# A Fourier-and-mixer kernel: fold pieces in two quarters only, a new setup order, and finer last stores

## The chip, the cores and the metric

The kernel runs on 1 core of one Trainium2 chip. The metric is the device time of one launch in microseconds (us), smaller is better; it is the median of repeated runs. A profile is of one execution and has a span (first to last recorded event) that is a little shorter than the time of that execution.

## The reference

The input x is 8 batches of 3008 rows (tokens) by 256 features, in fp32. Its two-dimensional Fourier transform over rows and features is taken and its real part goes through one mixer block with weights over tokens and over channels:

```python
x = np.fft.fft(np.fft.fft(x, axis=1), axis=2).real
xt = x.transpose(0, 2, 1)
h = np.maximum(xt @ w_tok1, 0.0) @ w_tok2     # 3008 -> 256 -> 3008
u = x + h.transpose(0, 2, 1)
h2 = np.maximum(u @ w_ch1, 0.0) @ w_ch2       # 256 -> 1536 -> 256
return u + h2                                  # fp32
```

## The kernel before

**The work per batch.** The transform over 3008 rows is split into 64 times 47. `load_x` (L155) brings a batch in as `xp` and, gathered by an indirect DMA, as the mirrored rows `xm`. `fold` (L445) adds each row's mirror to it (`xp` add, L457) and makes even and odd halves over the features (`eo` add L461, `eo` subtract L463), in four parts of three pieces: 12 pieces a batch, all on VectorE; the first piece has two small ones beside it (L455, L456). `front` (L561) is a generator of the transform and the token mixing: `inner` and `outer` products into `z`, twelve `pw` products into `w` (L587, L588, combined on VectorE at L590), then in `rest` (L596) the products with the token weights `tok1` (L601, part 0 from `hp`, part 1 from `hq`), the sums of the two parts (`part_q` on ScalarE, `units` on VectorE), the relu into `uu`, and `third` (L631), which finishes the transform in `yt`. The chunk loop (L680) then makes, for each of six chunks of 512 tokens and two halves of 128 features, `pu` = token weights times `uu` in two products, and `ut` = `pu` + `yt` in one VectorE add (L704); the view `"p (b a) -> p a b"` turns the order of the tokens on the way.

**The channel part.** `mm1` (L728) multiplies a chunk of `ut` with the first channel weights (`wc1p` or its mirror `wc1m`) into twelve `pc` banks, and ScalarE writes the relu to `c1` (L739). The second channel product is done by `mm2_sums` (L764) in seven products of quarter size for eight; it needs block sums of `c1` (`block_sums`, L743, four adds for each half of the blocks) and of the weights (`wst`). It runs in four quarters s = 0 to 3, and its residuals (L762) are added to the output tile `osb` by VectorE, and by POOL at the end of quarters 0 and 3. Chunk 0 of batch 0 and the last chunk of an even batch and of the last batch take the plain path (`mm2`, L817: twelve products into `po` per 128 tokens).

**The order.** The schedule is written out by hand: each engine runs its instructions in the order of the program. Banks of PSUM come from three pools, `f` with three, `mm` with three and `o2` with two; setup code takes them in turn from a ring over all (`ps_any`, L79). The main loop (L930) goes over batches b, chunks c and quarters s; sub = 4c + s is the sub-step. In each it issues three `mm1` blocks of this chunk, some pieces of this batch's front (`own_plan`), some of the next one's (`nxt`, by `plan`), one quarter of `mm2` of the previous chunk, and by `fold_plan` a piece of the fold of batch b + 2 (for b = 1, of batch 2 and then 3). The inner function `now()` (L945) issues block sums: those of the previous chunk's second half at s = 0 and 1, of this chunk's first half at s = 2 and 3. In batch 0 `align_w2` copies the token weights into the aligned `w2p` on ScalarE, piece by piece; `early` is the fold of batch 1.

**The setup** (L874 to 914) makes the sine tables `tp` and `tq` (ScalarE), transposes them (`turn_in`, `turned_out`), reverses their rows (`turn_rows`), multiplies them with the token weights (`carried`, six groups for `hp`, six for `hq`), and meanwhile does batch 0's fold (`fold0`) and front (`zw0`, `mirrored` for the mirror column of `w`, then `rest(0)`). `filler(n)` issues n products of 128 columns whose result isn't used; `warm(24)` is the like, of 256 columns, at the start. DMAs for weights go out on POOL's queue (`gdma`, `gather`); outputs and the transposes of `ut` (`turn_u`) on SP's.

Of the kernel before, what the change touches and what calls it, by code (L numbers as in the profile page):

```python
# [41 lines left out]
def kernel(  # L42
# [24 lines left out]
    def ps_mm(name):  # L67
        return psum.tile([P, 512], FP32, tag="mm", name=name, bufs=3)

    def ps_out(name):  # L70
        return psum.tile([P, 512], FP32, tag="o2", name=name, bufs=2)
# [6 lines left out]

    def ps_any(name, dt=FP32, n=512):  # L79
        tag, bufs = next(ring)  # L80
        return psum.tile([P, n], dt, tag=tag, name=name, bufs=bufs)
# [176 lines left out]
    def turn_in(tab):  # L258
        pts = []
        for h in range(2):  # L260
            pt = ps_any("pt", FP16, 1024)
            for g in range(6):
                nc.tensor.transpose(out=pt[:, g * P:(g + 1) * P],
                                    in_=tab[:, 6 * h + g, :], identity=ident[:])
            pts.append(pt)
        return pts
# [5 lines left out]
    def turn(tab, tts, warm):  # L272
        turned_out(tts, turn_in(tab))
        filler(warm)
# [321 lines left out]
    def rest(b):  # L596
# [63 lines left out]
        else:  # L660
            third(0)
            yield
            pts = [ps_out("pt1") for _ in range(2)]
            for th in range(2):
                tok1(pts[th], th, 0)
            yield
            sqs = []
            for th in range(2):
                tok1(pts[th], th, 1)
                sqs.append(part_q(pts[th]))  # L670
            uvs = [units(pts[th], sqs[th]) for th in range(2)]
            relu(0, uvs[0], (0,))
            for h in range(2):
                nc.scalar.activation(out=uu[:, 1, 0, h, :], in_=uvs[1][:, h, :],
                                     func=AFT.Relu)
            for th in range(2):
                relu(th, uvs[th], (1, 2))
            yield
        uts = st["ut"] = []
        for c in range(NCH):  # L680
# [10 lines left out]
            uts.append(ut)  # L691
            for h in range(2):
# [124 lines left out]
    def mm2(b, c, c1, ks, box):  # L817
# [15 lines left out]
        for ct in range(NCT if n else 0):  # L833
            nc.tensor.matmul(po[0:n, o:o + D], lhsT=c1[:, ct, ks * P:ks * P + n],  # L834
                             rhs=wc2[:, ct, :],
                             start=(ct == 0), stop=(ct == NCT - 1))
        if ks % 2 == 1 or final:
# [9 lines left out]
        first = 2 if final and ks == 3 else 0  # L847
        if ks == 3 or (final and ks == 1):
            for i in range(2):
                nk = min(ks + 1, 3 if last and (i or n == 0) else 4)  # L850
                eng = nc.scalar if i and final else nc.sync
# [4 lines left out]
            if ks == 3 and last and b % 2:  # L856
                nc.sync.dma_start(
# [18 lines left out]
    turn(tp, tts_p, 16)  # L876
# [9 lines left out]
    turned_out(tts_q, turn_in(tq))  # L886
    for g2, e in enumerate((1, 1)):
        carried(tts_p, hp, g2, e)
    table_perm()
    take(own, 4)  # L890
    carried(tts_p, hp, 2, 0)
# [7 lines left out]
    carried(tts_q, hq, 0, 0)  # L899
    mirrored(state[0]["w"], ps_any("pt1"))  # L900
    own = front(0)
    carried(tts_q, hq, 1, 1)
    take(own, 1)
    carried(tts_q, hq, 2, 0)
    take(own, 1)
    carried(tts_q, hq, 3, 1, ps_mm)
    carried(tts_q, hq, 4, 0, ps_mm)
    carried(tts_q, hq, 5, 0, ps_mm)
    take(own, 3)
    tables_folded()  # L910
    filler(12)
# [14 lines left out]
    fold_plan = [[0] * 15 + [1] * 9] + [[0] * 10 + [1] * 12 + [0, 0]] * (BB - 1)  # L926
    fold_plan[1] = [1, 1, 1] + fold_plan[1][3:]
    prev = None
    turned_u = {(0, 0): turn_u(0, 0)}
    for b in range(BB):  # L930
# [3 lines left out]
        for c in range(NCH):  # L934
# [6 lines left out]
            for s in range(4):  # L941
# [13 lines left out]
                take(nxt, n // 2)  # L955
# [4 lines left out]
                if s == 2:  # L960
                    now()
                if b == 0 and sub < 16 and sub % 2:
                    align_w2(sub // 2)
                take(nxt, n - n // 2)
                if s == 1:
                    now()
# [55 lines left out]
```

## Time and profile before

| what | value |
|---|---|
| three runs, us | 606.51, 605.36, 606.27 (median 606.27) |
| profiled execution, us | 605.55 |
| its span, us | 603.8 |
| granted TensorE clock, mean | 1.00 |
| DMA moved, MB (mean GB/s) | 56.53 (94) |
| fold pieces: `xp` add L457, `eo` add L461, `eo` subtract L463, mean ns | 768, 695, 618 (28 each) |
| block sum L753, mean ns of its four forms | 598, 564, 567, 554 (84 each) |
| TensorE busy in 0 to 33, 33 to 100, 100 to 530, 530 to 604 us | 23.98, 65.78, 430.00, 69.21 |
| VectorE busy in the same | 26.50, 53.52, 330.13, 43.67 |

PE is TensorE's matmul, PEld its weight load, DVE VectorE, ACT ScalarE, POOL GpSimd, SP SyncE; a q behind a name is the engine's queue of DMA issues and semaphore waits. A line of the page's group list has the source line, the engine, the operation, output<-input by the program's names, the shape and the count, then the busy time and the mean ns of one. A line of the timeline has the start in us, the duration in us of the whole group of like instructions, engine, line, operation, output<-input, shape, count, and in brackets how long the engine stood idle before it and which instruction's end released it. Matmuls are pipelined: the duration of one (219 ns for 128 columns) is longer than the time from its start to the next one's. Row names leave numbers out, so that `c` is `c1`, `pt` is `pt1` and `wc` is `wc2`.

### The profile page before, as it was taken

Reading aid. Unit: us, or ns where it says so; the run is one execution under the profiler, and the core shown is the slowest. Engines: PE = TensorE matmul, PEld = TensorE weight load, DVE = VectorE, ACT = ScalarE, POOL = GpSimd, SP = SyncE. Lnnn points to the kernel's source line nnn. Section 1 sums busy time; section 2 is a strip of 40 time slices with the busy share of each in tenths; the row PEclk is TensorE's granted clock in tenths of the full one; section 3 lists DMA queues with packets and bytes.
Section 4 is the critical chain, followed back from the end, with each engine's and each line's share of the span. In section 5 each row is a group of like instructions: output and inputs, shape, how many; then the busy total and the mean of one; then the engine's idle time right before and its main releaser. Section 6 shows DMA issues by size and latency. Waiting matters only on the chain.

```text
span 603.8 us, 15712 instructions
## 1 busy us (share of the span) xinstructions
PE 589.0 (98%) x6323; PEld 421.3 (70%) x6323; DVE 453.8 (75%) x1022; ACT 436.7 (72%) x983; POOL 146.0 (24%) x234
## 2 busy tenths in 40 slices
PE   4999999999999999999999999999999999999996
PEld 3846677666877677767777667766777677766675
DVE  8788697669796798657988589756989666766572
ACT  8776985777777776687777777777776877767772
POOL 7500412311341121311223212401221121111131
PEclk9999999999999999999999999999999999999999
DMA  9994761693467223952429332482232424232423
GB/s 153 210 202 117 111 104 37 113 157 57 66 113 143 53 63 80 150 72 65 96 46 169 87 71 55 94 163 53 55 88 44 82 53 93 51 71 65 85 60 99
DMA packets 86665, 56.53 MB, mean 94 GB/s; under 512 B 54928, under 2 KB 83536, under 8 KB 85840
## 3 DMA queue, kind: packets, MB, share of 16 engines
q1 hardware_dynamic: 78048, 37.84, 32.9%
q0 software_dynamic: 8320, 17.49, 16.9%
q8 instruction: 49, 0.80, 0.5%
q14 instruction: 24, 0.20, 0.1%
q10 hardware_dynamic: 224, 0.20, 0.1%
HBM read 34.98 MB, written 24.64 MB: 99 GB/s over the span
## 4 chain that ended last, share of the span: by engine, by line
PE 93%; DVE 3%; ACT 3%; issue 0%; DVEq 0%; POOL 0%; POOLq 0%
PE pc L736 39%; PE px L777 23%; PE py L777 9%; PE pu L696 7%; PE po L834 4%; PE pt L604 4%; PE pz L509 1%; PE pq L636 1%; PE py L636 1%; PE pw L588 1%; PE pw L587 1%; DVE sb L753 1%; ACT c L739 0%; PE pw L551 0%; DVE osb L762 0%
## 5 line engine op out<-in xcount | busy, mean ns | idle before, releaser
L739 ACT ACTIVATE c<-pc 128x512 f16<-128x512 f32 (+1 forms) x572 | 295.8, 594 | 38.1 <-PE pc L736 20.1
L762 POOL TENSOR_TENSOR osb<-osb,rt 128x256 f32<-128x256 f32 x84 | 79.5, 946 | 367.7 <-DVE osb L762 360.6
L736 PE MATMUL pc<-ut,wc1p 128*128 128x512 f16 x576 | 140.5, 379 | 0.0
L777 PEld LDWEIGHTS <-c 128*128 128x128 f16 x2016 | 121.4, 98 | 21.6 <-issue 1.8
L736 PE MATMUL pc<-ut,wc1m 128*128 128x512 f16 (+1 forms) x576 | 134.9, 370 | 0.0
L704 DVE TENSOR_TENSOR ut<-pu,yt 128x512 f16<-128x512 f32 (+1 forms) x96 | 64.6, 675 | 51.9 <-PE pu L696 51.7
L782 ACT ACTIVATE m<-px 128x256 f32<-128x256 f32 x126 | 48.5, 385 | 68.2 <-PE px L777 44.2
L777 PEld LDWEIGHTS <-sb 128*128 128x128 f16 x1512 | 90.0, 98 | 10.4 <-issue 0.7
L736 PEld LDWEIGHTS <-wc1p 128*128 128x128 f16 x576 | 52.2, 98 | 49.2 <-issue 2.6
L736 PEld LDWEIGHTS <-wc1m 128*128 128x128 f16 x576 | 52.9, 98 | 46.5
L777 PE MATMUL px<-wst,c 128*128 128x128 f16 x1008 | 70.9, 219 | 0.6 <-DVE c L753 0.6
L777 PE MATMUL px<-wc,c 128*128 128x128 f16 x1008 | 63.1, 219 | 0.3 <-DVE osb L762 0.3
L753 DVE TENSOR_TENSOR sb<-sb,c 128x768 f16<-128x768 f16 x84 | 50.3, 598 | 2.9
L305 ACT ACTIVATE z<-pz 128x480 f16<-128x480 f32 (+1 forms) x60 | 40.0, 672 | 16.9 <-PE pz L509 11.1
L762 DVE TENSOR_TENSOR osb<-py,m 128x256 f32<-128x256 f32 x84 | 35.2, 419 | 21.0 <-ACT m L782 19.5
L696 PE MATMUL pu<-w2p,uu 128*128 128x512 f16 (+1 forms) x168 | 49.8, 379 | 0.0
L753 DVE TENSOR_TENSOR sb<-c 128x768 f16<-128x768 f16 x84 | 47.4, 564 | 2.0 <-ACT c L739 2.0
L753 DVE TENSOR_TENSOR sb<-c,sb 128x768 f16<-128x768 f16 x84 | 47.6, 567 | 0.0
L753 DVE TENSOR_TENSOR c<-c 128x768 f16<-128x768 f16 x84 | 46.5, 554 | 0.0
L590 DVE SCALAR_TENSOR_TENSOR w<-alt,pw 128x131 f16<-128x131 f16 x84 | 29.4, 351 | 18.1 <-ACT w L305 17.4
L643 DVE TENSOR_TENSOR yt<-py,qs 128x512 f16<-128x512 f32 x48 | 30.9, 686 | 15.7 <-ACT qs L639 14.9
L777 PE MATMUL py<-wst,sb 128*128 128x128 f16 x504 | 35.2, 219 | 0.1
(184 smaller groups left out, 681.0 us busy)
## 6 DMA issues: line engine op xcount, KB each, us to landing
out_dram<-osb SPq DMA_DIRECT2D x83, 256.0 KB, 3.6
xp<-in_x_dram POOLq DMA_DIRECT2D x16, 272.0 KB, 5.5
out_dram<-osb SPq DMA_DIRECT2D x11, 192.0 KB, 3.2
xp<-in_x_dram POOLq DMA_DIRECT2D x16, 127.5 KB, 6.3
rt<-ut SPq DMA_TRANSPOSE x96, 3.9
w2s<-in_moe_w_tok_dram POOLq DMA_DIRECT2D x1, 1504.0 KB, 14.5
w1p<-in_moe_w_tok_dram POOLq DMA_DIRECT2D x4, 192.0 KB, 7.8
wc<-in_moe_w_ch_dram POOLq DMA_DIRECT2D x1, 768.0 KB
```

What stands on the lines that cost most here:

```text
L305: nc.scalar.activation(out=out_, in_=in_, func=AFT.Copy)
L590: nc.vector.scalar_tensor_tensor(out=w[:, g, 0:131], in0=alt[:], scalar=pw[:, 131:132], in1=pw[:, 0:131], op0=AT.mult, op1=AT.add)
L604: nc.tensor.matmul(pt[:, o:o + n], lhsT=hw[:, g, th * P:th * P + P], rhs=w[:, g, f:f + n], start=(g == 0), stop=(g == NG - 1))
L643: nc.vector.tensor_tensor(out=yt[:, h, CW * c:CW * c + CW], in0=py[:], in1=qs[:], op=op)
L696: nc.tensor.matmul(pu[:, 0:n], lhsT=uu[:, th, int(minus), h, :], rhs=w2_cols(b, c)[:, th], start=(th == 0), stop=(th == 1))
L704: nc.vector.tensor_tensor(out=ut[:, h, 0:n].rearrange("p (a b) -> p a b", b=64), in0=pu[:, 0:n].rearrange("p (b a) -> p a b", b=64), in1=y ...
L736: nc.tensor.matmul(pc[:, 0:n], lhsT=wc[:, h, ct * P:(ct + 1) * P], rhs=ut[:, h, 0:n], start=(h == 0), stop=(h == 1))
L739: nc.scalar.activation(out=c1[:, ct, 0:n], in_=pc[:, 0:n], func=AFT.Relu)
L753: nc.vector.tensor_tensor(out=o, in0=x, in1=y, op=op)
L762: eng.tensor_tensor(out=o, in0=x, in1=y, op=AT.add)
L777: nc.tensor.matmul(o[:, t], lhsT=a(k)[:, f:f + P], rhs=w(k), start=(first and t == 0 and k == 0), stop=(k == HC - 1), skip_group_check=True)
L782: nc.scalar.activation(out=m[:, i], in_=pa[:, 0], func=AFT.Copy)
```

## The change

1. **Setup order.** `tq` is transposed right after `tp`, into the two `o2` banks, which the ring then leaves out (`held`) until ScalarE has copied them; the 16 fillers there become 12 and 4, and the 12 before the main loop go. The first `hp` groups are evicted in a slightly different order. Groups 1 to 3 of `hq` now stand between `mirrored` and `third(0)`, groups 4 and 5 between `third(0)` and the first `tok1` products; some evictions change engine.
2. **Batch 0's token mixing and chunk 0.** ScalarE copies part 0 of `tok1` to `sp`, and VectorE subtracts and adds part 1 from PSUM. The four relus come in the order th 0, th 1. In chunk 0 `yt` is added in PSUM, by a product with the identity matrix whose output is written in the order `(b a)`, strided; VectorE and ScalarE then copy one half each to `ut`.
3. **Fold pieces.** `fold_plan` puts one piece at s = 0 and two at s = 1, none at s = 2 and 3; in batch 0 the pieces (2, 2, 1, 0, 2, 2) come at sub-steps 16 to 21. `load_x(b + 3)` comes at sub-step 22, `load_x(3)` at 1 of batch 1.
4. **Block sums.** At s = 1 `now()` comes right after `mm2`, ahead of the next front's pieces, and both of these come after `mm2`.
5. **Last stores.** In the last chunk the last 128 tokens are computed in two halves of 128 features, each with its residual at once; tokens of ks = 2 are stored by themselves, and the last store goes on ScalarE's queue.

```diff
@@ -76,8 +76,10 @@
     ring = cycle((("f", 3), ("mm", 3), ("o2", 2), ("f", 3), ("mm", 3), ("f", 3), ("mm", 3),
                   ("o2", 2)))
 
+    held = set()
+
     def ps_any(name, dt=FP32, n=512):
-        tag, bufs = next(ring)
+        tag, bufs = next(r for r in ring if r[0] not in held)
         return psum.tile([P, n], dt, tag=tag, name=name, bufs=bufs)
 
     def dram(t, offset, ap):
@@ -255,10 +257,10 @@
         return [stage.tile([P, NG * P], FP16, tag="tt", bufs=4, name="tt")
                 for _ in range(2)]
 
-    def turn_in(tab):
+    def turn_in(tab, pool=ps_any):
         pts = []
         for h in range(2):
-            pt = ps_any("pt", FP16, 1024)
+            pt = pool("pt", FP16, 1024)
             for g in range(6):
                 nc.tensor.transpose(out=pt[:, g * P:(g + 1) * P],
                                     in_=tab[:, 6 * h + g, :], identity=ident[:])
@@ -660,21 +662,27 @@
         else:
             third(0)
             yield
-            pts = [ps_out("pt1") for _ in range(2)]
+            uvs, sps = [], []
             for th in range(2):
-                tok1(pts[th], th, 0)
+                pt = ps_mm("pt1")
+                tok1(pt, th, 0)
+                sp = perb.tile([P, 130], FP32, tag="sp", name="sp", bufs=2)
+                nc.scalar.activation(out=sp[:], in_=pt[:, 0:130], func=AFT.Copy)
+                uv = perb.tile([P, 2, P], FP32, tag="uv", name="uv", bufs=2)
+                nc.vector.tensor_copy(out=uv[:, :, 0], in_=sp[:, 0:130:129])
+                sps.append(sp)
+                uvs.append(uv)
             yield
-            sqs = []
             for th in range(2):
-                tok1(pts[th], th, 1)
-                sqs.append(part_q(pts[th]))
-            uvs = [units(pts[th], sqs[th]) for th in range(2)]
-            relu(0, uvs[0], (0,))
-            for h in range(2):
-                nc.scalar.activation(out=uu[:, 1, 0, h, :], in_=uvs[1][:, h, :],
-                                     func=AFT.Relu)
+                pt = ps_out("pt1")
+                tok1(pt, th, 1)
+                for h, op in ((0, AT.subtract), (1, AT.add)):
+                    nc.vector.tensor_tensor(out=uvs[th][:, h, 1:P], in0=sps[th][:, 2:129],
+                                            in1=pt[:, 130:257], op=op)
             for th in range(2):
-                relu(th, uvs[th], (1, 2))
+                for h in range(2):
+                    nc.scalar.activation(out=uu[:, th, 0, h, :], in_=uvs[th][:, h, :],
+                                         func=AFT.Relu)
             yield
         uts = st["ut"] = []
         for c in range(NCH):
@@ -689,6 +697,25 @@
             elif n < CW:
                 nc.vector.memset(ut[:, :, n:CW], 0.0)
             uts.append(ut)
+            if (b, c) == (0, 0):
+                pus = [ps_f("pu") for _ in range(2)]
+                for h in range(2):
+                    nc.tensor.matmul(pus[h][:].rearrange("p (b a) -> p a b", b=64),
+                                     lhsT=ident[:],
+                                     rhs=yt[:, h, 0:CW].rearrange("p (a b) -> p a b", b=64),
+                                     start=True, stop=False)
+                for th in range(2):
+                    for h in range(2):
+                        nc.tensor.matmul(pus[h][:], lhsT=uu[:, th, 0, h, :],
+                                         rhs=w2_cols(b, c)[:, th],
+                                         start=False, stop=(th == 1))
+                for h in range(2):
+                    copy(1 - h, ut[:, h, :].rearrange("p (a b) -> p a b", b=64),
+                         pus[h][:].rearrange("p (b a) -> p a b", b=64))
+                for th in range(2):
+                    relu(th, uvs[th], (1, 2))
+                yield
+                continue
             for h in range(2):
                 minus = c >= 3
                 pu = ps_f("pu")
@@ -830,11 +857,17 @@
             box["po"] = ps_out("po")
         po = box["po"]
         o = D * (ks % 2)
-        for ct in range(NCT if n else 0):
-            nc.tensor.matmul(po[0:n, o:o + D], lhsT=c1[:, ct, ks * P:ks * P + n],
-                             rhs=wc2[:, ct, :],
-                             start=(ct == 0), stop=(ct == NCT - 1))
-        if ks % 2 == 1 or final:
+        w = P if final and ks == 3 else D
+        for d in range(0, D if n else 0, w):
+            for ct in range(NCT):
+                nc.tensor.matmul(po[0:n, o + d:o + d + w],
+                                 lhsT=c1[:, ct, ks * P:ks * P + n],
+                                 rhs=wc2[:, ct, d:d + w],
+                                 start=(ct == 0), stop=(ct == NCT - 1))
+            if final and ks == 3:
+                j, p = ((lower, lower), (upper, turned_))[d // w]
+                residual(nc.vector, osb[:, 3, j], po[:, o + d:o + d + w], rt[:, 3, p])
+        if ks % 2 == 1 and not final or final and ks < 3:
             src = po[:].rearrange("p (k d) -> p k d", k=2)
             parts = [(slice(0, P), 0, 2)] if n == P else [(slice(0, P), 0, 1),
                                                           (slice(0, n), 1, 2)]
@@ -844,17 +877,19 @@
                 ks_ = slice(ks - ks % 2 + k0, ks - ks % 2 + k1)
                 for j, p in ((lower, lower), (upper, turned_)):
                     residual(nc.vector, osb[r, ks_, j], src[r, k0:k1, j], rt[r, ks_, p])
-        first = 2 if final and ks == 3 else 0
-        if ks == 3 or (final and ks == 1):
+        first = ks if final and ks > 1 else 0
+        if ks == 3 or (final and ks):
             for i in range(2):
                 nk = min(ks + 1, 3 if last and (i or n == 0) else 4)
+                if nk == first:
+                    continue
                 eng = nc.scalar if i and final else nc.sync
                 eng.dma_start(
                     out=dram(out_t, (b * S + 8 * c + i + 2 * first) * D,
                              [[NQ * D, 64], [2 * D, nk - first], [1, D]]),
                     in_=osb[64 * i:64 * i + 64, first:nk, :])
             if ks == 3 and last and b % 2:
-                nc.sync.dma_start(
+                (nc.scalar if final else nc.sync).dma_start(
                     out=dram(out_t, ((b - 1) * S + NQ - 1) * D, [[NQ * D, 64], [1, D]]),
                     in_=osb[64:P, 3, :])
 
@@ -873,7 +908,11 @@
 
     warm(24)
     table3(tq, vq, (shift0[:], shift1[:]))
-    turn(tp, tts_p, 16)
+    held.add("o2")
+    turned_out(tts_p, turn_in(tp, ps_mm))
+    filler(12)
+    pts_q = turn_in(tq, ps_out)
+    filler(4)
     table_d()
     pieces = fold0()
     take(pieces, 5)
@@ -883,12 +922,12 @@
     take(own, 3)
     table_b()
     take(own, 3)
-    turned_out(tts_q, turn_in(tq))
-    for g2, e in enumerate((1, 1)):
+    turned_out(tts_q, pts_q)
+    held.clear()
+    for g2, e in enumerate((1, 1, 0)):
         carried(tts_p, hp, g2, e)
     table_perm()
     take(own, 4)
-    carried(tts_p, hp, 2, 0)
     turn_rows(tts_q, -1.0, 0)
     take(own, 3)
     carried(tts_p, hp, 3, 1)
@@ -896,19 +935,16 @@
     carried(tts_p, hp, 4, 0)
     take(own, 2)
     carried(tts_p, hp, 5, 1)
-    carried(tts_q, hq, 0, 0)
+    carried(tts_q, hq, 0, 1)
     mirrored(state[0]["w"], ps_any("pt1"))
     own = front(0)
-    carried(tts_q, hq, 1, 1)
+    for g2, e in ((1, 0), (2, 1), (3, 0)):
+        carried(tts_q, hq, g2, e)
     take(own, 1)
-    carried(tts_q, hq, 2, 0)
-    take(own, 1)
-    carried(tts_q, hq, 3, 1, ps_mm)
-    carried(tts_q, hq, 4, 0, ps_mm)
-    carried(tts_q, hq, 5, 0, ps_mm)
+    for g2, e in ((4, 1), (5, 0)):
+        carried(tts_q, hq, g2, e)
     take(own, 3)
     tables_folded()
-    filler(12)
     load_wc2()
     if BB > 1:
         x_tiles[1] = load_x(1)
@@ -923,8 +959,9 @@
                 [1, 1, 1, 0, 0, 1, 1, 0, 1, 1, 0, 0, 1, 1] + [0] * 10]
     own_plan += [[1, 1, 1, 0, 0, 1, 1, 0, 1, 1, 0, 0, 1, 1] + [0] * 10] * (BB - 2)
     early_plan = [0] * 4 + [2, 2, 1, 2, 1, 2, 2] + [0] * 13
-    fold_plan = [[0] * 15 + [1] * 9] + [[0] * 10 + [1] * 12 + [0, 0]] * (BB - 1)
-    fold_plan[1] = [1, 1, 1] + fold_plan[1][3:]
+    fold_plan = [[0] * 8 + [1, 2, 0, 0] * 4 for _ in range(BB)]
+    fold_plan[0] = [0] * 16 + [2, 2, 1, 0, 2, 2, 0, 0]
+    fold_plan[1] = [1, 2, 0, 0] + [0] * 4 + [0, 2, 0, 0] + [1, 2, 0, 0] * 2 + [1, 2, 1, 0]
     prev = None
     turned_u = {(0, 0): turn_u(0, 0)}
     for b in range(BB):
@@ -952,18 +989,17 @@
                 if s == 3:
                     now()
                 take(own, own_plan[b][sub])
-                take(nxt, n // 2)
+                first = 0 if s == 1 else n // 2
+                take(nxt, first)
                 if s == 0:
                     now()
                 if prev is not None:
                     mm2(*prev, s, pbox)
-                if s == 2:
+                if s in (1, 2):
                     now()
                 if b == 0 and sub < 16 and sub % 2:
                     align_w2(sub // 2)
-                take(nxt, n - n // 2)
-                if s == 1:
-                    now()
+                take(nxt, n - first)
                 if s == 2 and c + 1 < NCH:
                     turned_u[b, c + 1] = turn_u(b, c + 1)
                 if s == 3 and c + 1 == NCH and b + 1 < BB:
@@ -977,12 +1013,12 @@
                     if sub == 10:
                         x_tiles[2] = load_x(2)
                 if folds is not None and fold_plan[b][sub]:
-                    take(folds, 1)
-                    if b == 1 and sub == 2:
+                    take(folds, fold_plan[b][sub])
+                    if b == 1 and sub == 1:
                         x_tiles[3] = load_x(3)
                         folds = fold(3, [nc.vector] * 4)
-                    elif sub == 21 and b and b + 3 < BB:
-                        x_tiles[b + 3] = load_x(b + 3)
+                if sub == 22 and b and b + 3 < BB:
+                    x_tiles[b + 3] = load_x(b + 3)
             if c + 1 == NCH and b % 2 == 0:
                 pair(b, c1)
             prev, pbox = (b, c, c1), box
```

More of the change, by code (lines that the diff above doesn't have):

```diff
@@ L65, with ps_mm, ps_out @@
         tc.tile_pool(name="psump", bufs=1, space=bass.MemoryType.PSUM))
[L67 to L71, printed above, removed]
+    def ps_mm(name, dt=FP32, n=512):
+        return psum.tile([P, n], dt, tag="mm", name=name, bufs=3)
+    def ps_out(name, dt=FP32, n=512):
+        return psum.tile([P, n], dt, tag="o2", name=name, bufs=2)
     def ps_f(name, dt=FP32, n=512):
```

## The prediction

> **What bounds the kernel now.** I read the page first, its shares of busy time and then the chain that ended last:
>
> ```profile
> PE 589.0 (98%) x6323; PEld 421.3 (70%) x6323; DVE 453.8 (75%) x1022; ACT 436.7 (72%) x983; POOL 146.0 (24%) x234
> ...
> PEclk9999999999999999999999999999999999999999
> ...
> PE 93%; DVE 3%; ACT 3%; issue 0%; DVEq 0%; POOL 0%; POOLq 0%
> ```
>
> TensorE is busy 98% of the span and is 93% of the chain. By starts of neighbouring matmuls, 128 columns take 55.7 ns, 256 take 109 and 512 take 216; the columns of all matmuls need 559.1 us at 2.4 columns a ns, so only some 45 us are open to any schedule. Taking the starts apart in stretches of 20 us, what is lost against 1/2.4 ns a column is 5.1 us in 0 to 20, 2.9 in 20 to 40, 0.9, 1.5 and 2.5 in the next three, then 0.6 to 1.1 in each (about 1.1 per batch of 72 us). A change that leaves the big products alone can win in three places: the setup, batch 0 and the end. I read each in the timeline.
>
> Setup, TensorE, then VectorE:
>
> ```profile
> 13.88 0.60 PE L509 MATMUL pz<-t1n,xp 94*128 94x96 f16 x10 [1.35 <-DVE xp L479]
> ...
> 24.95 0.40 PE L636 MATMUL pq<-tq,w 128*128 128x128 f16 x4 [0.34 <-ACT w L526]
> ...
> 29.43 0.96 PE L604 MATMUL pt<-w,hq 128*128 128x127 f16 x14 [0.18 <-ACT hq L305]
> 31.12 1.33 PE L696 MATMUL pu<-w2s,uu 128*128 128x512 f16 x4 [0.73 <-ACT uu L627]
> 32.29 0.83 PE L298 MATMUL filler<-ident 128*128 128x128 f16 x12
> 32.96 1.37 PE L736 MATMUL pc<-ut,wc1p 128*128 128x512 f16 x5
> ```
> ```profile
> 30.07 0.16 DVE L615 COPY uv<-pt 128x2 f32<-128x2 f32 x1 [1.52 <-ACT sq L610]
> ...
> 31.96 1.29 DVE L704 TENSOR_TENSOR ut<-pu,yt 128x512 f16<-128x512 f32 x2 [0.67 <-PE pu L696]
> ```
>
> From the last `tok1` product (its last issue ends near 30.2) to `pc` at 32.96 nothing useful is issued but four `pu`: a relay copy, subtract, relu, product, two adds. In batch 0 three products wait for VectorE:
>
> ```profile
> 82.64 0.83 PE L777 MATMUL px<-wst,sb 128*128 128x128 f16 x12 [0.25 <-DVE osb L762]
> ...
> 90.06 1.50 PE L777 MATMUL px<-wc,c 128*128 128x128 f16 x24 [0.28 <-DVE osb L762]
> ...
> 99.53 0.68 PE L777 MATMUL px<-wst,c 128*128 128x128 f16 x9 [0.57 <-DVE c L753]
> ```
>
> The end is one residual and two stores in a row on SP's queue:
>
> ```profile
> 599.25 0.49 DVE L762 TENSOR_TENSOR osb<-po,rt 128x128 f32<-128x128 f32 x2 [0.82 <-PE po L834]
> 599.76 0.60 SPq L852 DMA_DIRECT2D out_dram<-osb  x1
> 600.41 0.60 SPq L857 DMA_DIRECT2D out_dram<-osb  x1
> ```
>
> **The change, part by part.** The sum is made against the profiled execution, 605.55 us (span 603.8, so 1.75 us around it); that is 0.72 below the median of 606.27, so my total is added to the median.
>
> *Setup, up to the last `tok1`.* The twelve `tq` transposes (12 x 55.7 ns = 0.67 us) move from 16.88 into the 1.35-us wait before 13.88, in place of 16 fillers that are split 12 and 4; their two banks are held, so nothing is evicted earlier. This alone wins little: ScalarE, which must copy them out (1.57 us from 17.82), has its own order of copies there, and I find `pw` only some 0.1 us earlier. But three `hq` groups (12 x 109 ns = 1.3 us) now stand between the mirror column and `third(0)`: they cover the wait at 24.95 (0.50 us by starts). With the last two groups split over two engines, the 0.34-us gap by starts at 29.43 shrinks to about 0.15. So 0.1 + 0.5 + 0.2 = 0.8 us: the last `tok1` issue ends at 29.4. What moves on POOL and SP here is nothing; the transfers keep their order.
>
> *Setup, the relay.* Before, 30.2 to the effective second `pc` product at 33.30: 3.1 us. After, part 0 is copied by ScalarE under part 1 (hidden by 24 matmuls); VectorE subtracts straight from PSUM (0.28 us each, 0.2 apart), four relus (0.25 each) end near 30.4, then four `pu` products at the row of the strided read (264 ns between starts) with one copy each on VectorE (0.69) and ScalarE (0.60) in parallel, where two adds of 0.65 were in series. That gives the first `pc` at 31.5 and the second near 31.7. The fillers (0.67 us) go; they lay in this wait and cost nothing. But another thing is late next: the gathered half of `wc1p` is issued at 15.74 and takes 16.1 us to land, 31.8, while the queue moves some 200 GB/s without a pause. So the second `pc` cannot start before about 31.86: 33.30 - 31.86 = 1.44 us for the whole setup.
>
> *The identity products.* `yt` is now added in PSUM by two 512-column products whose output walks with a stride of 32 bytes. No row of before writes PSUM that way. The nearest is the strided read `pu<-w2s`: 264 ns between starts against 216 for the aligned `w2p`, 48 ns more. By it the two cost 0.53 us, and they lie before the relus are done, where about 0.4 us is free: 0.1 us on the path, inside the slack that the landing of `wc1p` leaves. The Trainium skill speaks against it: "PSUM — Partial Sum Buffer", Specifications (TRN2), says that PSUM has 8-byte cachelines and that any access pattern that isn't contiguous slows matmuls significantly, without a figure. If I take "significantly" as four times (an assumption), the two cost 1.7 us, 1.3 more, and after the slack 1.1 us of the 1.44 is lost. I take the row, as it is a product of the same size with the same stride pattern, and keep 0.2 to 1.6 us as the bounds of the setup. A gain beyond that is excluded by the landing.
>
> *Relus and column copies for later chunks* now come after chunk 0's copies on ScalarE (0.9 us in before); `pc`'s own relus queue behind, and the next user is chunk 3, so nothing waits.
>
> *Folds.* A fold piece of two SBUF inputs runs long when POOL adds a residual at the same time: 0.42 us alone, 1.42 beside POOL's 1.16 us:
>
> ```profile
> 140.97 1.42 DVE L461 TENSOR_TENSOR eo<-xp 94x512 f16<-94x512 f16 x1
> ```
>
> Now one `xp` piece (0.68) stands at quarter 0 and two `eo` pieces at quarter 1, none at 2 and 3. POOL's 0.67-us residual follows quarter 0's own, so each `xp` piece meets it (0.68 to about 1.17), and `eo` pieces stay at 0.42. VectorE has a quarter of its time free, so that is hidden unless a product waits for a bank behind it. In batch 0 the waits at 82.64 and 90.06 mostly become shorter or move to quarter 0, and the 0.57 at 99.53 (0.74 by starts) goes, because the sums of quarter 1 now precede `uv` and `yt` on VectorE. Against this, at sub-step 13 both outer products come after `px`, so ScalarE's `z` copies come behind `m` and one `w2p` copy: the next `pw` is 0.3 to 0.5 late. 0.4 of the first two waits and 0.7 of the third, less 0.4 and about 0.2 for the moved wait: net 0.5 us; bounds -0.3 to +1.2.
>
> *Batches 1 to 7.* They lose 1.1 us each, of which 0.157 is the wait for `yt` behind ScalarE's `qs`, which the change leaves. The `px` waits after a late sum come to 0.57 us in all and partly go; new ones may come where a fold pair stands ahead of `w` or `ut`. No row shows them: I take a gain of 0.2 us, bounds -0.8 to +1.0. The loads of x are issued one sub-step (3 us) later on POOL and are used a third of a batch later: nothing waits.
>
> *End.* The last group of twelve 256-column products is cut in two of twelve 128-column ones: 24 x 55.7 - 12 x 109 = 0.03 us more. The first half's residual lies under the second half, one of 0.28 us remains instead of 0.49, and the two last stores go on two queues side by side. Before, the last store is issued at 600.41 and lands 2.1 us later; after, at about 599.6: gain 0.75 us, bounds 0.5 to 0.9.
>
> Sum: 1.44 + 0.5 + 0.2 + 0.75 = 2.9 us. Profiled execution 602.65, and on the median 606.27 - 2.9 = 603.4.
>
> **The rivals.**
> A. The setup gain is held back: the strided PSUM write is slow as the page has it, or ScalarE's chain or the gathered weights come later. Then 0.3 of the 1.44 stays, and the sum is 1.75: 604.5. For it: the sentence quoted, and a queue full to 44 us. Against: the 48 ns of the strided read.
> B. The folds give more. The 1.1 us lost per batch is then mostly collisions of fold pieces with POOL; with a quarter of it gone in seven batches, 7 x 0.25 = 1.75 us more than I took: 601.7. For it: `eo` averages 0.70 where 0.42 is possible. Against: no wait above 0.16 us in these batches.
> C. Slower. The doubled `eo` pair at quarter 1 (0.84 us, and 1.17 of `xp` ahead of it) makes VectorE late for `w`, `ut` or the residual before a bank is reused, in each of some 24 pairs. It has to cost 2.9 us before it is even, and 4.1 to be seen as slower: 24 x 0.17. At 0.2 us each, 4.8 us, the time is 608.2. For it: in batch 0 exactly such lateness costs 0.25 to 0.57. Against: between 100 and 530 us TensorE is busy 430.0 of 430.0, with VectorE at 330.
> D. The parts don't add up: ScalarE's chain holds the setup as before and the batches cancel, so only the end and part of the relay stay, about 1.0: 605.3, which is no difference (0.2%, 1.2 us, is about what a measurement of this kernel can tell from no change).
>
> **How the numbers follow.** My forecast, 602.6 to 604.2, has 0.45; A, 604.2 to 605.1, has 0.22; B, 601.0 to 602.6, has 0.20; D 0.09; C 0.04. The predicted time is the likeliest's, 603.4. For 8 in 10 the range takes in most of A and of B: 601.4 to 605.2. Faster by over 0.2% (below 605.06): 0.45 + 0.22 + 0.20 and 0.02 of D = 0.89. Within it: 0.08, from D and the mild end of C. Slower: 0.03.
>
> **What will show it.** The first `pc` starts near 31.5 and the second product near 31.9; the start before them of the two identity products is 264 ns from the next, or 800 if the page's sentence decides. The waits near 24.95 and 99.53 are gone, and one near 73 is new. `eo` averages below 0.5 us and `xp` near 1.1. The last store is issued before 599.7 less the setup's and batch 0's gain, and lands 2.1 us after. I am wrong if TensorE's loss in batches 1 to 7 leaves 0.8 to 1.3 us each, or if the first `pc` comes after 32.3.

## The result, and the profile after

The changed kernel takes 602.27 us (median of 4 runs, 602.22 to 602.50) against 606.29 for the kernel before on the same chip: a ratio of 0.9937, 95% interval 0.992 to 0.9955, so 4.0 us less. The profiled executions differ by 3.05 us (605.55 and 602.50), and a second comparison further down gives 0.9956 (0.9942 to 0.9969), 2.6 us. The kernel before has two levels (on one chip 43 of 51 runs lie between 605.05 and 605.56 and 8 between 605.9 and 606.7), and the first comparison met the upper one in three of four, so the gain to explain is the 3.0 us of the traces.

The page of the changed kernel, its shares and its chain, the same lines as before:

```profile
PE 588.6 (98%) x6325; PEld 421.7 (70%) x6325; DVE 449.7 (75%) x1022; ACT 436.5 (73%) x984; POOL 141.2 (23%) x234
...
PE 94%; DVE 3%; ACT 2%; issue 0%; POOL 0%; DVEq 0%; POOLq 0%
```

It looks as before, which says that the shares can't tell this change. What tells it is where TensorE lost time, by the starts of neighbouring matmuls (each against its columns at 2.4 a ns plus about 2.6 ns):

| us lost in | before | changed | sums and folds alone (e9) | sums alone (e2) | folds alone (e3) |
|---|---|---|---|---|---|
| 0 to 33 | 6.98 | 6.29 | 6.94 | 7.01 | 6.93 |
| 33 to 104 | 3.53 | 2.66 | 2.65 | 3.08 | 3.23 |
| 104 to 590 | 7.28 | 6.12 | 6.11 | 6.48 | 8.13 |
| from 590 on | 0.06 | 0.60 | 0.06 | 0.06 | 0.06 |

Matched by the order of the `pc` products, the changed kernel is ahead by 0.98 us at the first `pc`, 1.79 at the start of batch 1, 2.95 near 490 us, and 3.05 at the end of the span. So setup 0.98 (0.93 at the second `pc`; the fillers that went did no useful work, so this is more than the first row), batch 0 0.81 to 0.87, batches 1 to 7 1.16, the end 0.10. Some 0.2 to 0.3 us of the 1.16 is not the change's: e1 and e4 below run these batches as the kernel before does, and are 0.22 and 0.31 us ahead of its profiled execution there.

The end of the setup on TensorE:

```profile
29.40 1.02 PE L703 MATMUL pu<-yt,ident 128*128 128x512 f16 x2
30.21 1.25 PE L709 MATMUL pu<-w2s,uu 128*128 128x512 f16 x4
31.98 1.64 PE L763 MATMUL pc<-ut,wc1p 128*128 128x512 f16 x6 [0.52 <-DVE ut L305]
```

The two identity products take 0.81 us of issue for 1024 columns. The weight loads of the same stretch show the landing that comes after them:

```profile
PEld L763 <- DMA wc1p<-in_moe_w_ch_dram,ixc: 1.2, 1, 1.2
```

By single starts the second `pc` comes at 32.37, 389 ns after the first instead of 216: it waited 0.17 us for the gathered half of `wc1p`. In batch 0 one wait for VectorE is left between 79 and 92 us:

```profile
89.01 1.50 PE L804 MATMUL px<-wc,c 128*128 128x128 f16 x24 [0.65 <-DVE osb L789]
```

The waits near 82 and 99 us are gone, and this one has grown from 0.28. The end has a wait that the kernel before doesn't have:

```profile
593.80 1.82 PE L863 MATMUL po<-wc,c 128*128 128x256 f16 x21
596.00 0.83 PE L863 MATMUL po<-wc,c 128*128 128x128 f16 x12 [0.38 <-DVE osb L789]
```

The last twelve products wait for the residual of the first half (0.54 us by starts).

### The profile page after: what moved, and what is told of

Same layout as the page of the kernel before. It is cut to its first block, busy times and chain, and to the rows that moved or that the text cites. A ratio compares the mean times of both kernels' runs of the same rounds, so it can differ in the third digit from the quotient of the medians.

```text
span 600.7 us, 15716 instructions
## 1 busy us (share of the span) xinstructions
PE 588.6 (98%) x6325; PEld 421.7 (70%) x6325; DVE 449.7 (75%) x1022; ACT 436.5 (73%) x984; POOL 141.2 (23%) x234
## 4 chain that ended last, share of the span: by engine, by line
PE 94%; DVE 3%; ACT 2%; issue 0%; POOL 0%; DVEq 0%; POOLq 0%
PE pc L763 40%; PE px L804 23%; PE py L804 9%; PE pu L723 7%; PE po L863 4%; PE pt L606 4%; PE pz L511 2%; PE py L638 1%; PE pq L638 1%; PE pw L589 1%; PE pw L590 1%; ACT z L307 1%; PE pw L553 0%; DVE sb L780 0%; ACT tt L307 0%; PE ph L428 0%
## 5 line engine op out<-in xcount | busy, mean ns | idle before, releaser
L731 DVE TENSOR_TENSOR ut<-pu,yt 128x512 f16<-128x512 f32 (+1 forms) x94 | 63.3, 674 | 46.8 <-PE pu L723 46.0
L780 DVE TENSOR_TENSOR c<-c 128x768 f16<-128x768 f16 x84 | 48.1, 572 | 0.0
L592 DVE SCALAR_TENSOR_TENSOR w<-alt,pw 128x131 f16<-128x131 f16 x84 | 29.4, 351 | 20.2 <-ACT w L307 20.2
L804 PE MATMUL py<-wc,sb 128*128 128x128 f16 x504 | 35.0, 219 | 0.0
```

Of the source, the lines that this page charges most:

```text
L592: nc.vector.scalar_tensor_tensor(out=w[:, g, 0:131], in0=alt[:], scalar=pw[:, 131:132], in1=pw[:, 0:131], op0=AT.mult, op1=AT.add)
L731: nc.vector.tensor_tensor(out=ut[:, h, 0:n].rearrange("p (a b) -> p a b", b=64), in0=pu[:, 0:n].rearrange("p (b a) -> p a b", b=64), in1=y ...
L780: nc.vector.tensor_tensor(out=o, in0=x, in1=y, op=op)
L804: nc.tensor.matmul(o[:, t], lhsT=a(k)[:, f:f + P], rhs=w(k), start=(first and t == 0 and k == 0), stop=(k == HC - 1), skip_group_check=True)
```

## The experiments

My theory after this: setup about 0.95 us, the order of the sums nearly all of the batches' gain, the fold plan near nothing, the stores near nothing because of the wait just shown. The main rival: the fold plan carries the batches. I took the parts one by one first, each on the kernel before, then altered the changed kernel. Medians of 5 to 21 runs; the kernel before stood at 605.23 (e1 to e4), 605.31 (e5 to e8) and 605.38 (e9 to e11).

| run | us | ratio to before, 95% interval |
|---|---|---|
| e1 setup alone | 604.29 | 0.9988 (0.9980 to 0.9996) |
| e2 order of the sums alone | 604.25 | 0.9986 (0.9979 to 0.9993) |
| e3 fold plan and loads alone | 606.05 | 1.0011 (1.0004 to 1.0019) |
| e4 last stores alone | 605.14 | 1.0002 (0.9994 to 1.0010) |
| e5 the changed kernel again | 602.70 | 0.9956 (0.9942 to 0.9969) |
| e6 other bank at the end | 601.82 | 0.9944 (0.9930 to 0.9958) |
| e7 identity products read strided | 603.12 | 0.9967 (0.9955 to 0.9979) |
| e8 gather in two halves | 602.71 | 0.9959 (0.9945 to 0.9973) |
| e9 sums and folds together | 603.45 | 0.9965 (0.9952 to 0.9979) |
| e10 chunk 0 with adds | 602.83 | 0.9951 (0.9937 to 0.9964) |
| e11 folds of batch 0 spread, other bank | 602.84 | 0.9954 (0.9940 to 0.9968) |

**e1, setup alone.** The hunks of the diff that are about the setup order, the `tok1` parts and chunk 0.

> The setup part alone on the kernel before: the new order, the copies of part 0, the identity products and the two-engine copy of chunk 0; folds, block sums and last stores as before. If the parts add up as the two traces suggest, it takes 0.9 to 1.0 us off (first pc near 32.0 instead of 32.96) and nothing later changes: 605.3. Rival: the two traces differ in the setup by chance of the DMA (the gathered weights land 0.5 us later in the changed kernel's run), then the gain is up to 1.4 us with the second pc near 31.9; or the gain is lost at the next wait of batch 0, then below 0.5 us.

Measured: 0.94 us off. At the median the setup is worth what the traces said, and nothing later takes it back. But its profiled execution (604.82) was 0.53 us slower than that, and there the second `pc` comes at 32.78, only 0.53 us sooner than before. The trace names a wait that none of my theories had: a product of the fourth `hp` group starts at 21.68, 0.53 us late, behind the landing of `w1m`, a part of the token weights. The weight loads of e10 and of e11 show the same:

```profile
PEld L428 <- DMA w1m<-in_moe_w_tok_dram: 0.7, 1, 0.7
PEld L428 <- DMA w1m<-in_moe_w_tok_dram: 0.5, 1, 0.5
```

By starts it costs 0.40 us in e5, 0.60 in e10, 0.48 in e11 and 0.07 in the profile after; in e6 and e7, and in the five profiles with the old setup, it is not there. What delays the landing stays open.

**e2, the order of the sums alone.**

```diff
-                take(nxt, n // 2)
+                first = 0 if s == 1 else n // 2
+                take(nxt, first)
...
-                if s == 2:
+                if s in (1, 2):
                     now()
...
-                take(nxt, n - n // 2)
-                if s == 1:
-                    now()
+                take(nxt, n - first)
```

> Only the order is changed: the block sums of quarter 1 come ahead of the next front's pieces, and those of quarter 1 after the second channel product. Theory: this removes the 0.75 us wait near 99 us and the three waits of 0.06 to 0.10 us in each later batch, so about 0.75 + 7 x 0.17 = 1.9 us: 604.4. Rival: the small waits go by the fold plan, since fold pieces of quarters 2 and 3 stand ahead of residuals; then only 0.75 us: 605.5.

Measured: 0.98 us off, between the two. The wait near 99 us is gone. The kernel before also has three kinds of small waits in the later batches, of 0.09 to 0.10 us each by starts: `px` for a late sum (six times), `px` after `pu` (five times), and a third before another `px` (three times). Here the first kind goes. VectorE in the kernel before, then in this run:

```profile
134.46 0.35 DVE L590 SCALAR_TENSOR_TENSOR w<-alt,pw 128x131 f16<-128x131 f16 x1 [1.23 <-ACT w L305]
134.74 0.55 DVE L753 TENSOR_TENSOR c<-c 128x768 f16<-128x768 f16 x1
135.20 0.55 DVE L753 TENSOR_TENSOR sb<-c,sb 128x768 f16<-128x768 f16 x1
```
```profile
132.72 0.55 DVE L753 TENSOR_TENSOR c<-c 128x768 f16<-128x768 f16 x1
133.19 0.55 DVE L753 TENSOR_TENSOR sb<-c,sb 128x768 f16<-128x768 f16 x1
134.04 0.36 DVE L590 SCALAR_TENSOR_TENSOR w<-alt,pw 128x131 f16<-128x131 f16 x1 [0.30 <-ACT w L305]
```

The sums no longer stand behind a `w` that waits for ScalarE. The second kind stays in all five places and the third in two; the third is there only once in e1 and in e4, which leave these batches as they were, so it comes and goes from one execution to the next.

**e3, the fold plan alone.** The hunks of `fold_plan`, of `load_x` and of the number taken.

> Only the places of the fold pieces and of the loads of x are changed. Theory (order of the sums carries the batches): within 0.3 us of the kernel before, with a wait of about 0.8 us instead of 0.44 near 89 us in batch 0 and the waits near 82 us gone: 606.2. Rival (fold plan carries them): 1.2 us off or more, and the three small waits per batch gone: 605.0.

Measured: 0.82 us slower, which neither theory had. The second and third kind of small wait do go here, and the first stays. But TensorE now waits before the last of the twelve `tok1` products of part 0. VectorE, then TensorE, in this run:

```profile
156.10 0.55 DVE L753 TENSOR_TENSOR c<-c 128x768 f16<-128x768 f16 x1
156.57 0.55 DVE L753 TENSOR_TENSOR sb<-c,sb 128x768 f16<-128x768 f16 x1
157.04 0.68 DVE L457 TENSOR_TENSOR xp<-xp,xm 94x1020 f16<-94x1020 f16 x1
157.76 0.43 DVE L461 TENSOR_TENSOR eo<-xp 94x512 f16<-94x512 f16 x1
158.10 0.34 DVE L590 SCALAR_TENSOR_TENSOR w<-alt,pw 128x131 f16<-128x131 f16 x1
```
```profile
157.23 0.79 PE L604 MATMUL pt<-w,hp 128*128 128x130 f16 x11
158.50 0.22 PE L604 MATMUL pt<-w,hp 128*128 128x130 f16 x1 [0.47 <-DVE w L590]
```

The twelfth `w` is combined only behind two block sums and two fold pieces. The wait is 0.64 us by starts in batch 1 and 0.24 in each of the next four, where it was 0.11; another of 0.48 is new at 177 us, where `px` waits for a residual that VectorE makes behind a fold piece and two sums. In the changed kernel the same place reads:

```profile
154.31 0.36 DVE L592 SCALAR_TENSOR_TENSOR w<-alt,pw 128x131 f16<-128x131 f16 x1
154.58 0.68 DVE L459 TENSOR_TENSOR xp<-xp,xm 94x1020 f16<-94x1020 f16 x1
155.30 0.43 DVE L463 TENSOR_TENSOR eo<-xp 94x512 f16<-94x512 f16 x1
156.05 0.35 DVE L592 SCALAR_TENSOR_TENSOR w<-alt,pw 128x131 f16<-128x131 f16 x1 [0.32 <-ACT w L307]
```

The sums of that quarter have already been done, the fold pieces end 0.32 us before `w` can start, and the wait is 0.11 again. The one near 177 us is down to 0.18, in e9 too. So the fold pieces are nearly covered, but only with the new order of the sums.

**e4, the last stores alone.**

> Only the last stores are changed. Theory: the second half of the last group waits 0.54 us for the residual of the first half, since both lie in one bank, so 0.1 to 0.2 us off: 606.1. Rival (the prediction): no wait there, 0.75 us off: 605.5.

Measured: 0.09 us off, inside the noise. The same wait (0.55 us by starts) ends at 598.57 in its trace. The prediction's step for the end is refuted.

**e5, the changed kernel again**, on one chip with e6 to e8.

> The changed kernel itself, once more and beside the next three on one chip. If it takes 3.0 us off, as the profiles say (605.55 to 602.50), it is at 602.2 where the kernel before is at 605.2; the parts alone then leave 1.8 us unexplained (0.94 + 0.98 - 0.82 + 0.09 = 1.2). If it takes only about 1.2 us off here, the parts add up and the first comparison was off.

Measured: 2.6 us off, its runs from 602.23 to 603.26. The parts e1 to e4 sum to 1.2 us, so they do not add up; e9 says which two depend on each other.

**e6, another bank for the second half.**

```diff
         for d in range(0, D if n else 0, w):
+            if final and ks == 3 and d:
+                po = ps_out("po")
             for ct in range(NCT):
```

> The changed kernel with the second half of the last group written to another PSUM bank than the first. Theory: the 0.54 us wait of that half for the residual of the first is a matter of the shared bank and goes: 0.5 us below the changed kernel. Rival: the stores in flight decide the end, then 0.1 us or less.

Measured: 601.82, 0.9 us below e5 (the intervals against the kernel before overlap), of which the trace shows 0.54 at this place. The sixty last products run without a gap:

```profile
589.86 0.83 PE L804 MATMUL py<-wc,sb 128*128 128x128 f16 x12
590.59 5.43 PE L865 MATMUL po<-wc,c 128*128 128x256 f16 x60
```

The rest of the 0.9 is in the setup (second `pc` at 32.12, in e5 at 32.55): e5's profiled execution has the wait of 0.40 us for `w1m`, this one doesn't. From the last `pc` on, this run is 0.63 us ahead of the kernel before, where the changed kernel is 0.10 ahead. The edit gives the second half another tile as well as another bank; which of the two the products wait by is not separated.

**e7, identity products that read strided and write contiguously.**

```diff
-pus[h][:].rearrange("p (b a) -> p a b", b=64)
+pus[h][:].rearrange("p (b a) -> p b a", b=64)
...
-rhs=yt[:, h, 0:CW].rearrange("p (a b) -> p a b", b=64)
+rhs=yt[:, h, 0:CW].rearrange("p (a b) -> p b a", b=64)
```

> The changed kernel with the identity products turned round: they read yt with a stride of 128 bytes and write PSUM contiguously; the result is the same. Theory: the strided write is what made them 386 and 429 ns between starts; now 264 ns or less each, and the first pc starts 0.25 to 0.3 us earlier. If the gathered weights land last, the second pc still waits for them and the time falls by 0.1 us or less; if the chain of the identity products decides, by 0.25 us. Rival: the identity products are slow for another reason (the first matmuls into a bank that was read): no change.

Measured: 0.4 us slower than e5, so the theory is refuted. The products got slower still:

```profile
29.34 1.88 PE L703 MATMUL pu<-yt,ident 128*128 128x512 f16 x2
31.05 1.23 PE L709 MATMUL pu<-w2s,uu 128*128 128x512 f16 x4
```

They take 1.71 us to the next start, 0.86 each, four times the contiguous 216 ns. Single elements of 2 bytes at steps of 128 bytes are not what `w2s` is, which comes in runs of eight; the row that I took as nearest was not near. From the last `tok1` product (29.29) to the second `pc` (33.01) it is 3.72 us here and 2.85 in e5, so the strided read costs 0.87; e5's execution had lost 0.40 of that earlier, at `w1m`.

**e8, the gather in two halves of the columns.** Two gathers of 768 columns in place of one, with their own indices computed on POOL.

> The changed kernel with the gather of wc1p in two halves of the columns, so that the half that the first products need lands about 0.9 us sooner. Theory: the second pc no longer waits for the landing (0.17 us in the profile): 0.15 to 0.2 us less, more in executions whose transfers come later. Rival: the extra gather on POOL delays the loads behind it and the time stays or rises.

Measured: 602.71, no change against e5. It decides little: the index arithmetic let POOL issue the first gather at 18.6 us instead of 16.7, and in e5's own execution the second `pc` (32.55) did not wait for the landing.

**e9, sums and folds together on the kernel before.**

> The order of the sums and the fold plan together on the kernel before; setup and last stores as before. Theory (the two depend on each other: the fold pairs fit only once the sums no longer stand ahead of the last w): batch 0 gives 0.87 and the later batches 1.16 us as in the trace of the changed kernel, so 2.0 us off, 603.2. Rival (they add up): 0.98 off and 0.82 on, 605.1.

Measured: 1.93 us off, where the two apart make 0.16. Its losses in the table are those of the changed kernel in batch 0 and in the later batches. Sums and folds depend on each other. With e1 (0.94) and e4 (0.09) the sum is 2.96 us.

**e10, chunk 0 with products and adds as before.** The block for chunk 0 is taken out, the rest of the setup stays.

> The changed kernel without the identity products: chunk 0 is made as in the kernel before, two products and one VectorE add for each half, one add after the other; everything else as changed. If the identity products with their strided output and the two-engine copy are what shortens the way to the second pc, it now starts 0.6 us later: 603.2. If the slow strided writes eat what the parallel copies give, it starts within 0.1 to 0.2 us of the changed kernel's: 602.6 to 602.8.

Measured: 602.83, against 602.70 for e5 on another chip (intervals overlap). Its end of the setup:

```profile
30.20 0.43 PE L704 MATMUL pu<-w2s,uu 128*128 128x512 f16 x1
30.88 0.96 PE L704 MATMUL pu<-w2s,uu 128*128 128x512 f16 x3 [0.25 <-ACT uu L684]
32.09 0.38 PE L749 MATMUL pc<-ut,wc1p 128*128 128x512 f16 x1 [0.25 <-DVE ut L712]
32.69 0.81 PE L749 MATMUL pc<-ut,wc1p 128*128 128x512 f16 x3 [0.22 <-DVE ut L712]
```

The last `tok1` product starts at 29.94 here, so it is 2.75 us to the second `pc`; with the identity products it is 2.85 in e5 and e6 (29.70 to 32.55, 29.27 to 32.12) and 3.03 in the profile after. The products with the identity and the parallel copies together bring nothing. By the traces the setup's gain comes from the new order (last `tok1` product at 30.18 before, at 29.34 in the profile after) and from the shorter relay before `uu` (3.12 us from there to the second `pc` before, 2.75 here).

**e11, fold pieces of batch 0 spread, with the other bank of e6.**

```diff
-    fold_plan[0] = [0] * 16 + [2, 2, 1, 0, 2, 2, 0, 0]
+    fold_plan[0] = [0] * 15 + [1, 1, 1, 1, 0, 0, 2, 2, 1]
```

> The changed kernel with the second half of the last group in another bank, and the nine fold pieces of batch 0 spread out: one each at sub-steps 15 to 18, two at 21 and 22, one at 23. Theory: VectorE's backlog at sub-steps 16 to 18 is what makes px wait 0.8 us near 88 us; the wait falls to 0.3 us or less, and the time to 601.3 (the other bank alone stood at 601.8). Rival: the wait is made by the two sums at quarter 3 and stays; 601.8.

Measured: 602.84, no better than the changed kernel and 1.0 above e6, with runs from 602.13 to 604.10. The three waits of the kernel before come back:

```profile
82.70 0.68 PE L804 MATMUL py<-wst,sb 128*128 128x128 f16 x9 [0.20 <-DVE sb L780]
83.63 0.83 PE L804 MATMUL px<-wst,sb 128*128 128x128 f16 x12 [0.25 <-DVE osb L789]
...
91.15 0.55 PE L804 MATMUL px<-wc,c 128*128 128x128 f16 x7 [0.28 <-DVE osb L789]
```

By starts they cost 0.37, 0.41 and 0.44 us, 1.22 together, against 0.82 in one wait. My theory that a flatter spread relieves VectorE there is refuted. The rest is something else: in its profiled execution (604.10) the second `pc` waited 0.9 us for the gathered weights, an `hp` product 0.48 for `w1m`, and a `px` at 59.19 0.41 for VectorE, which the profile after doesn't have. The two fastest of its five runs (602.13 and 602.17) are 0.3 to 0.4 us above e6, about what the waits of batch 0 say.

**e12, what a stride costs.** Eleven groups of eight identity products are appended; only their spacing is read, not the time of the run (648.5 us).

> The changed kernel followed by eleven groups of eight products with the identity, 512 columns each, on a warm clock: contiguous, then the output written in the order (b a) for b = 256, 128, 64, 16, 4 (strides of 8, 16, 32, 128, 512 bytes), then the input read with strides of 4, 8, 16, 64, 256 bytes in the same way. The outputs of the kernel stay. Theory: writes cost about 390 to 430 ns between starts at 32 bytes against 216 contiguous, and a read about 860 ns at 128 bytes; if the cost goes by PSUM's lines of 8 bytes, 8 bytes already costs the full factor of two and no stride more. Rival: it is a matter of the first products after another bank was in use, then in a row of eight all come down to 216.

One thing in that text was wrong: the inputs are read at strides of 512, 256, 128, 32 and 8 bytes for b = 256, 128, 64, 16, 4. The contiguous group and the five strided writes:

```profile
598.10 1.89 PE L1031 MATMUL probe<-wc,ident 128*128 128x512 f16 x8
599.83 3.60 PE L1033 MATMUL probe<-wc,ident 128*128 128x512 f16 x8
603.22 3.64 PE L1035 MATMUL probe<-wc,ident 128*128 128x512 f16 x8
606.65 3.64 PE L1037 MATMUL probe<-wc,ident 128*128 128x512 f16 x8
610.08 3.64 PE L1039 MATMUL probe<-wc,ident 128*128 128x512 f16 x8
613.52 3.64 PE L1041 MATMUL probe<-wc,ident 128*128 128x512 f16 x8
```

Eight contiguous ones take 1.73 us to the next start, 216 ns each; eight with a strided output 3.43, 429 ns each (the very first 387), whatever the stride from 8 to 512 bytes. So the factor of two is there at 8 bytes already, and the rival, that only the first products after another bank are slow, is out. The two in the changed kernel were exactly this, 386 and 429. The granted clock was 1.00 here; it fell to 0.82 and 0.50 in the later groups of strided reads, so of those only the 128-byte one (860 ns, at a clock of 0.50) is used, because e7 gives the same (842 and 861) at 1.00.

## Why the prediction was right, and where its steps were not

The forecast of 2.9 us holds against 3.0, but as a sum of terms that were off in both directions: setup and end gave 1.1 us less than forecast, the batches 1.3 more. That these cancel is luck. The predicted time, 603.4, is 1.1 us above the 602.27 measured, because it starts from a median of the upper level (606.27); for the profiled execution it was 602.65, and that took 602.50.

| step | predicted, us | measured, us | by |
|---|---|---|---|
| setup | 1.44 | 0.94 to 0.98 | median of e1, first `pc` in the two traces |
| batch 0 | 0.5 | 0.81 to 0.87 | the two traces |
| batches 1 to 7 | 0.2 | 1.16, some 0.9 against e1 and e4 | traces |
| end | 0.75 | 0.09 to 0.10 | e4, the two traces |

*Setup, up to the last `tok1`:* right in the profile after. Its last product starts at 29.34, predicted to end at 29.4, and the wait near 24.95 is gone. Not foreseen was the wait for `w1m`: with it the last product starts at 29.70 in e5 and at 29.94 in e10. The first `pc`, said to show the prediction wrong if it came after 32.3, is at 31.98 in the profile after and at 32.34 in e5.

*The identity products:* mis-sized. I took 264 ns by the row of the strided read and kept 864 as the other bound; it is 429. That is 0.28 us of the 0.48 by which the first `pc` came later than 31.5 (31.98). The rule of the Trainium skill, "PSUM — Partial Sum Buffer", Specifications (TRN2), was right in sign: a strided output is slow. Its size, a factor of two and no dependence on the stride, is what e12 shows; neither my row nor my reading of "significantly" had it.

*The landing of the gathered weights:* the right thing to look for, with a figure that moves. Predicted 31.8; in the profile after, the gather was issued 1.07 us later and the second `pc` started at 32.37; in e11, issued at 17.28, at 33.67; in e5 it did not wait. What moves POOL's issues and landings by more than 1 us from one execution to the next was not settled.

*Batch 0:* three of four steps right. The wait near 99 us (0.74 by starts) went, as argued, by the order of the sums; the one near 73 grew from 0.19 to 0.37. I had the waits near 82 and 90 us give 0.4 together. There were three, not two (one of 0.25 at 81.72 is not in my list): those at 81.72 and 82.64 went wholly (0.66), and the one at 90.06 grew from 0.44 to 0.82.

*Batches 1 to 7:* the failed step is "I take a gain of 0.2 us". Up to three waits of about 0.09 us per batch go, and my sum had counted only those for a late sum (0.57 us in all), as going in part. e2 and e3 show that the new order removes this kind and the fold plan the other two, and e9 that both together also keep most of e3's new waits away. What is left is 0.9 to 1.1 us per batch, inside the 0.8 to 1.3 that I had named; like the 1.1 before, it allows some 2.6 ns per product, which my figures per 20 us do not. The pieces are as predicted for `eo` (0.44 and 0.47 us mean instead of 0.70 and 0.62); `xp` rose only from 0.77 to 0.84, not to 1.1: 16 of 28 stay at 0.68 us, and 8 take 1.12 us or more, so most `xp` pieces do not meet POOL's addition.

*Rival A* was right that the strided write is slow and the gathered weights come later, but 0.94 of the 1.44 us stayed, not 0.3. *Rival B* has the measured 602.27 in its range: the folds and sums gave more, and `eo` is shorter as it said. But e2, which moves no fold piece, takes off the late sums alone (0.53 us in all). Whether the waits that the fold plan removes go because its pieces are shorter or because they stand elsewhere was not tested.

*Rival C* had a chance of 0.04, and e3 is that rival: the fold plan alone makes VectorE late for `w` and costs 0.8 us. What kept it out is the other half of the change, which I had costed apart. That VectorE "has a quarter of its time free" was no argument: the order in front of one instruction decided.

*End:* the failed step is "the first half's residual lies under the second half". Both halves lie in one tile and bank, and the second half's products wait for the residual that reads the first. e6 takes a second one, and the wait goes; its end gains 0.63 us, inside the bounds that I had set (0.5 to 0.9).

e6, the changed kernel with only its end mended, is the fastest of all kernels here (601.82).

## What to carry to other kernels

Two parts of a change that touch the order on one engine are costed together: here one was worth 1.0 us, the other -0.8, and both 1.9. With TensorE at 98%, waits below a tenth of a microsecond that came back batch after batch were most of what the later batches gave; list such waits without a threshold. Before an output is cut in pieces so that one is evicted under the next, look whether both lie in one tile and bank. When two executions of one kernel differ, look in both traces for the product that waits for a landing.

## What the runs showed of the hardware that I had not expected

A 512-column product with a strided fp32 output takes 429 ns between starts instead of 216, equally at strides of 8, 16, 32, 128 and 512 bytes. A product whose moving input is read in single 2-byte elements at 128 bytes takes 860 ns, while one read in runs of eight elements takes 264. Transfers issued by the same program landed early enough for nobody to wait in one execution and not in another: `w1m` cost the new setup 0 (e6, e7) to 0.60 us (e10), and the gathered weights held the second `pc` to 33.67 us in e11. I take these two to be much of what spreads the runs of the changed kernel (602.2 to 603.3 in e5); no run changes the landing alone, so this is not shown.
